# Keys transposed as two 64-row halves instead of one 128-row tile, in a gated linear attention and gMLP kernel

## The chip, the cores and the metric

The kernel runs on one NeuronCore of a Trainium2 chip. The metric is the device time of one execution in microseconds (us). Durations of single instructions are given in us or ns. The engines are PE (TensorE, matrix multiplies; its weight loads have rows of their own, PEld), DVE (VectorE), ACT (ScalarE), POOL (GpSimd) and SP (the queue that issues the DMAs). PE writes its results to PSUM, which has eight banks of 512 float32 columns in each partition; DVE and ACT carry them on to SBUF.

## The reference

There are 4 batches of 8 heads, 768 time steps and head size 48. The attention is a recurrence with a decay for each key dimension, and a gated MLP follows it:

```python
for t in range(S):                                             # q, k, v, alpha: (4, 8, 768, 48)
    state = alpha[:, :, t, :, None] * state + np.einsum('bhd,bhe->bhde', k[:, :, t], v[:, :, t])
    y[:, :, t] = np.einsum('bhd,bhde->bhe', q[:, :, t], state)
...
h = gelu(x @ w_in)                                             # x: y as (4, 768, 384); w_in: 384 x 1024
u, v = h[..., :512], h[..., 512:]
v_n = (v - mean(v)) / sqrt(var(v) + 1e-06) * g_ln
v_s = np.einsum('ts,bsd->btd', w_sg, v_n) + b_sg[None, :, None]
return x + (u * v_s) @ w_out
```

## The kernel before

The 768 steps of a batch are cut into 6 blocks of 128, so there are 24 blocks, numbered 0 to 23 here. The 8 heads stand as 4 pairs, and a pair takes 128 partitions, 64 for each of its heads (48 used). For block `i` DVE builds running products of the decays by two scans (`decay`, `invert`) and multiplies them into `q` and `k` (tile `kqv_t`).

What PE does for the attention comes in groups. Group `(o, i)` finishes the older block `o` and starts the newer block `i`, which is the next one. It has three steps, and on PE they stand one behind the other:

- `G` (`squares`): the scores of block `i` into tile `sc`, which has two PSUM banks, and the first part of the output `y` of block `o`. Block `o`'s contribution to the state goes to `dl0` (in the bank of tag `tp`) and to `dl1` (columns 256 to 447 of the second bank of `sc`).
- `M` (`squares_more`): the rest of block `o`'s output within the block, and the part from the old state `s_c`.
- `H` (`squares_end`): the part from the state at the middle of the block, `s_m`, and then, for block `i`, the transposes of the scaled keys. They are in float32, one of 128x128 for each of the four pairs, into the tile `tp`, which is one bank.

All matmuls of a group but the transposes are of 64x64, so that four of them run in the four quarters of the array at a time. `side_by_side` interleaves the lists of two row halves.

Around a group, DVE multiplies the scores by the causal mask (`causal`, tile `at`) and updates the state: `state_half` (`s_m`), then `state_add` and `state_decay` (`s_c`). ACT copies the transposed keys to SBUF (`k_rows`, tile `kn`), and the output to `xf` and `y3` (`x_rows`, `y_last`). Six small DMAs on SP then pack `y3` into `xf`, and ACT and DVE or POOL split `xf` into `xh` and `xl`, the operands of the MLP. Group `(i, i+1)` needs `at` and `kn` of block `i`.

The MLP is 128x128 work: `mm_v`, `mm_u`, `mm_s` and `mm_o` are its four products, in three passes each for float32 accuracy. The first 67 us also split the weights into two parts (`mm_w`).

The order of all this is made by a planner (`Plan`): every step is entered with its engine, a cost in ns, what it must follow, and the buffers it takes. `issue` then picks steps by their expected start and due time. The order on PE is mostly fixed by a list of units (`units`), in which the steps of a group are counted with the costs that `group` returns. The order on DVE, ACT, POOL and SP follows from the plan's costs. The framework under it adds semaphore waits: for data, and also between accesses by two engines to one PSUM tile; which of two such accesses waits is decided by the order in which the plan issued them.

Of the kernel before, what the change touches and what calls it, by code (L numbers as in the profile page):

```python
# [9 lines left out]
F32 = mybir.dt.float32  # L10
# [8 lines left out]
B, H, S, D = 4, 8, 768, 48  # L19
DM, DFF = 384, 1024  # L20
HALF = DFF // 2
P = 128
# [3 lines left out]
NP = H // 2  # L26
# [135 lines left out]
def tile_gla_gmlp(ctx: ExitStack, tc: tile.TileContext, aT, kqv, w_in, w_sgT, w_out, g_ln, b_sg, out):  # L162
    nc = tc.nc
# [4 lines left out]
    ps = ctx.enter_context(tc.tile_pool(name="ps", bufs=1, space=PSUM))  # L168
# [201 lines left out]
    def half(e):  # L370
        return slice(64 * e, 64 * e + 64)
# [34 lines left out]
    def gain_list(i, h):  # L406
# [6 lines left out]
            for j in range(NP) for e in range(2)  # L413
        ]

    def side_by_side(*slots):
        made = []
        for upper, lower in slots:
            for k in range(max(len(upper), len(lower))):
                made += [part[k]() for part in (upper, lower) if k < len(part)]  # L420
        return made
# [42 lines left out]
    def squares_end(o, i):  # L464
        if o is not None:
            side_by_side((inter_list(o, 1, 0), inter_list(o, 1, 1)))
        if i is not None:
            st[i]["tp"] = tp = ps.tile([P, NP, P], F32, tag="tp", name="tp")
            for j in range(NP):
                nc.tensor.transpose(tp[:, j], st[i]["k"][:, j], ident)  # L470

    def causal(i):
        s = st[i]
# [6 lines left out]
    def k_rows(i):  # L480
        s = st[i]
        s["kn"] = kn = att1.tile([P, NP, P], F32, tag="kn", name="kn")
        nc.scalar.copy(kn, s["tp"])

    def keep_warm(o, n):
        for _ in range(n):
# [253 lines left out]
    def group(o, i):  # L740
        i = i if i is not None and i < n else None
        name = ("G", o, i)
        if o is not None:
            o_at[o] = name
        if i is not None:
            s_at[i] = name
        first = [(name, 95 + SLOT * (2 if o is None else 3 if i is None else 5))]
        if o is not None:
            first.append((("M", o, i), 2 * SLOT))
        return first + [(("H", o, i), (0 if o is None else SLOT) + (0 if i is None else 530))]  # L750

    for i in range(NCH):
        units += group(i - 1 if i > 0 else None, i)
# [98 lines left out]
    for i in range(n):  # L852
# [14 lines left out]
        last = c == NCH - 1  # L867
        ended = ("H",) + o_at[i][1:]
        plan.add(("causal", i), "dve", 670, lambda i=i: causal(i), [s_at[i]], takes=[("at", 1, [o_at[i]])])
        plan.add(("kn", i), "act", 575, lambda i=i: k_rows(i), [("H",) + s_at[i][1:]], takes=[("kn", 1, [o_at[i]])])  # L870
        plan.add(
            ("half", i), "dve", 350, lambda i=i: state_half(i), [o_at[i]],
            lead={o_at[i]: SLOT * (0 if o_at[i][2] is None else 2)}, keen=400,
# [32 lines left out]
    for name, ns in units:  # L906
        if name[0] == "G":
# [2 lines left out]
            users = []  # L910
            if i is not None:
                deps += [("q", i), ("k", i)]
                users.append(("causal", i))
            if o is not None:
                deps += [("causal", o), ("kn", o)] + ([("state", o - 1)] if o % NCH > 0 else [])
                users += [("add", o)] if o % NCH < NCH - 1 else []
# [180 lines left out]
```

## Time and profile before

| | before |
|---|---|
| time, median of 3 runs | 375.91 us (375.25 to 377.3) |
| the profiled execution's own time | 374.54 us |
| its span in the trace | 372.8 us |
| mean granted PE clock | 0.988 |
| PE busy | 344.4 us, 92% |
| DVE busy | 265.1 us, 71% |
| ACT busy | 152.8 us, 41% |
| POOL busy | 60.6 us, 16% |

The profiled execution is 1.37 us under the median of the runs, and its time is 1.7 us more than its span. All single durations below come from that one execution. A row of a timeline gives the start, the length, the engine, the line, the operation, the tile written and the tiles read, and how many instructions the row merges; a bracket tells how long the engine had been idle and what released it.

### The profile page before, as it was taken

What the parts mean: (1) busy time and instruction counts of PE and PEld (TensorE: products, weight loads), DVE (VectorE), ACT (ScalarE), POOL (GpSimd) and SP (SyncE); (2) the same over time, 40 slices, a digit from 0 to 9 for tenths busy, and PEclk for the clock granted to TensorE, in tenths of its full rate; (3) what the DMA queues carried; (4) which work ended last, traced back from release to release, by engine and by line L of the source; (5) the groups of instructions that cost most, each with busy time, mean ns of one, the idle gap of its engine ahead of it and who ended that gap; (6) DMA issues with size and microseconds to landing.
All of it is one profiled execution on the core that took longest, in us unless ns stands there. A gap on an engine that the chain in (4) does not pass through costs nothing.

```text
span 372.8 us, 10703 instructions
## 1 busy us (share of the span) xinstructions
PE 344.4 (92%) x4480; PEld 314.3 (84%) x4480; DVE 265.1 (71%) x526; ACT 152.8 (41%) x367; POOL 60.6 (16%) x103
## 2 busy tenths in 40 slices
PE   2786989999998799999999999899999999999993
PEld 2554768799998798989999998699999989799983
DVE  4799997799996977888466887786577645443351
ACT  3285576755433344653312445543232335311010
POOL 1002133414201121320101301420111113300000
PEclk9999699999999999999999999999999999999998
DMA  8855675125356134531232344131221110000102
GB/s 304 281 195 139 218 250 181 42 73 163 98 170 205 31 111 122 162 114 37 66 117 93 119 138 136 52 101 28 92 83 73 30 50 8 1 2 0 63 3 70
DMA packets 18712, 39.38 MB, mean 106 GB/s; under 512 B 3936, under 2 KB 10848, under 8 KB 18656
## 3 DMA queue, kind: packets, MB, share of 16 engines
q1 hardware_dynamic: 18656, 38.61, 32.2%
q8 instruction: 37, 0.61, 0.7%
q14 instruction: 19, 0.16, 0.1%
HBM read 32.70 MB, written 4.72 MB: 100 GB/s over the span
## 4 chain that ended last, share of the span: by engine, by line
PE 68%; DVE 10%; DMA 8%; ACT 4%; SPq 4%; issue 3%; POOL 2%; DVEq 0%; ACTq 0%; POOLq 0%
PE mm_s L551 8%; PE mm_s L549 8%; PE mm_s L550 8%; DMA xf<-y 4%; PE mm_o L550 4%; PE mm_o L551 4%; PE mm_o L549 4%; PE mm_u L549 4%; SPq L520 4%; PE mm_u L551 4%; PE mm_u L550 4%; PE mm_v L549 3%; DMA kqv_t<-in_kqv 3%; PE mm_v L551 3%; PE mm_v L550 3%
## 5 line engine op out<-in xcount | busy, mean ns | idle before, releaser
L549 PE MATMUL mm_s<-ws_hi,vh 128*128 128x384 f32 x192 | 65.9, 343 | 1.3 <-ACT ws_hi L223 0.8
L550 PE MATMUL mm_s<-ws_lo,vh 128*128 128x384 f32 x192 | 65.1, 339 | 0.4 <-DVE ws_lo L226 0.4
L551 PE MATMUL mm_s<-ws_hi,vl 128*128 128x384 f32 x192 | 65.1, 339 | 0.1
L640 ACT CAST gh<-g 128x384 fp32r<-128x384 f32 x32 | 16.3, 512 | 57.9 <-DVE g L635 39.4
L630 DVE SCALAR_TENSOR_TENSOR g<-mm_s,g_col,b_bc 128x384 f32<-128x384 f32 x32 | 19.4, 608 | 26.1 <-PE mm_s L551 26.1
L549 PEld LDWEIGHTS mm_s<-ws_hi,vh 128*128 128x128 f32 x192 | 36.0, 188 | 2.1 <-ACT ws_hi L223 1.1
L550 PEld LDWEIGHTS mm_s<-ws_lo,vh 128*128 128x128 f32 x192 | 36.1, 188 | 0.8 <-DVE ws_lo L226 0.7
L551 PEld LDWEIGHTS mm_s<-ws_hi,vl 128*128 128x128 f32 x192 | 36.0, 188 | 0.4 <-DVE vl L596 0.4
L376 PE MATMUL sc<-kqv_t 64*64 64x64 f32 x768 | 27.8, 231 | 7.4 <-DVE kqv_t L361 4.7
L549 PE MATMUL mm_u<-xh,wi_hi 128*128 128x384 f32 x96 | 33.2, 346 | 0.1
L549 PE MATMUL mm_o<-gh,wo_hi 128*128 128x384 f32 x96 | 32.4, 338 | 0.3 <-ACT gh L640 0.3
L376 PEld LDWEIGHTS sc<-kqv_t 64*64 64x64 f32 x768 | 25.4, 146 | 8.5 <-DVE kqv_t L361 5.1
L550 PE MATMUL mm_o<-gl,wo_hi 128*128 128x384 f32 x96 | 32.4, 338 | 0.1
L550 PE MATMUL mm_u<-xl,wi_hi 128*128 128x384 f32 x96 | 32.5, 338 | 0.0
L551 PE MATMUL mm_u<-xh,wi_lo 128*128 128x384 f32 x96 | 32.4, 338 | 0.0
L551 PE MATMUL mm_o<-gh,wo_lo 128*128 128x384 f32 x96 | 32.3, 337 | 0.0
L549 PE MATMUL mm_v<-wi_hi,xh 128*128 128x512 f32 x72 | 30.3, 421 | 1.7 <-ACT u L615 1.4
L333 DVE TENSOR_TENSOR_SCAN pf<-a,floor 128x516 f32<-128x516 f32 x24 | 30.0, 1251 | 2.4 <-DMA a<-in_aT 2.2
L351 DVE TENSOR_TENSOR_SCAN pf<-a,floor 128x516 f32<-128x516 f32 x24 | 29.5, 1228 | 1.1 <-ACT pend L339 0.4
L551 PE MATMUL mm_v<-wi_hi,xl 128*128 128x512 f32 x72 | 28.5, 396 | 0.0
L550 PE MATMUL mm_v<-wi_lo,xh 128*128 128x512 f32 x72 | 28.4, 395 | 0.0
L389 PEld LDWEIGHTS y<-at,kqv_t 64*64 64x64 f32 x768 | 16.9, 141 | 13.2 <-issue 5.3
(109 smaller groups left out, 760.2 us busy)
## 6 DMA issues: line engine op xcount, KB each, us to landing
kqv_t<-in_kqv SPq DMA_DIRECT2D x24, 768.0 KB, 4.6
a<-in_aT SPq DMA_DIRECT2D x24, 258.5 KB, 2.7
out_x<-r SPq DMA_DIRECT2D x24, 192.0 KB, 2.5
raw<-in_w_in SPq DMA_DIRECT2D x8, 384.0 KB, 8.0
xf<-y SPq DMA_DIRECT2D x144, 8.0 KB, 2.7
raw<-in_w_out SPq DMA_DIRECT2D x4, 384.0 KB, 3.3
raw<-in_w_sgT SPq DMA_DIRECT2D x6, 192.0 KB, 2.4
raw_sg<-in_w_sgT SPq DMA_DIRECT2D x1, 768.0 KB
```

Source lines behind the costliest of these rows:

```text
L333: nc.vector.tensor_tensor_scan(pf.rearrange("p j t -> p (j t)"), s["a"][:, 0:NP * C1], floor.rearrange("p j t -> p (j t)"), initial=0.0, o ...
L351: nc.vector.tensor_tensor_scan(s["pf"].rearrange("p j t -> p (j t)")[:, ::-1], s["a"][:, NP * C1:0:-1], floor.rearrange("p j t -> p (j t)" ...
L376: lambda j=j, h=h: nc.tensor.matmul(sc[half(h), e, 64 * j:64 * j + 64], k[half(e), j, half(h)], q[half(e), j, half(h)], start=True, stop=True,
L389: lambda j=j: nc.tensor.matmul(y_of(y, j, e)[:, half(h)], v[half(h), j, half(e)], at[half(h), e, j], start=first and j < 2, stop=True, ski ...
L520: nc.sync.dma_start(xf[64 * e + D:64 * e + 64, kk, tsl], y3[64 * e + 16 * kk:64 * e + 16 * kk + 16, :])
L549: nc.tensor.matmul(o, lh, rh, start=(idx == 0), stop=False)
L550: nc.tensor.matmul(o, lh, rl, start=False, stop=False)
L551: nc.tensor.matmul(o, ll, rh, start=False, stop=(idx == n - 1))
L630: nc.vector.scalar_tensor_tensor(t["g"], t["o"], g_col[:, d:d + 1], b_bc[:, tsl], op0=ALU.mult, op1=ALU.add,)
L640: nc.scalar.copy(g["h"][:, d], t["g"])
```

## The change

Each pair's key tile is transposed in two halves by partition, 64 rows at a time. The upper half (head 0 of each pair) goes to `tp0`, which is columns 256 to 511 of the first bank of `sc`; the lower half goes to `tp1`, which is the old bank of tag `tp`. The two halves are interleaved, so that there are eight transposes of 64 rows to 128 output rows and 64 columns where there were four. `k_rows` copies them in two pieces, each 4x64 columns. In the plan, step `H` is counted with 260 ns in place of 530 for the transposes, the copy with 760 ns in place of 575, and the tile `sc` is held until `kn` is copied.

```diff
+    def rows_list(i, e):
+        k, tp = st[i]["k"], st[i]["tp1"] if e else st[i]["tp0"]
+        return [
+            lambda j=j: nc.tensor.transpose(tp[:, j], k[half(e), j], ident[half(e), half(e)]) for j in range(NP)
+        ]
+
...
-            st[i]["tp"] = tp = ps.tile([P, NP, P], F32, tag="tp", name="tp")
-            for j in range(NP):
-                nc.tensor.transpose(tp[:, j], st[i]["k"][:, j], ident)
+            st[i]["tp0"] = st[i]["sc"][:, 0, 256:512].rearrange("p (j d) -> p j d", d=64)
+            st[i]["tp1"] = ps.tile([P, NP, P], F32, tag="tp", name="tp")[:, :, 0:64]
+            side_by_side((rows_list(i, 0), rows_list(i, 1)))
...
-        nc.scalar.copy(kn, s["tp"])
+        nc.scalar.copy(kn[:, :, 0:64], s["tp0"])
+        nc.scalar.copy(kn[:, :, 64:P], s["tp1"])
...
-        return first + [(("H", o, i), (0 if o is None else SLOT) + (0 if i is None else 530))]
+        return first + [(("H", o, i), (0 if o is None else SLOT) + (0 if i is None else 260))]
...
-        plan.add(("kn", i), "act", 575, lambda i=i: k_rows(i), [("H",) + s_at[i][1:]], takes=[("kn", 1, [o_at[i]])])
+        plan.add(("kn", i), "act", 760, lambda i=i: k_rows(i), [("H",) + s_at[i][1:]], takes=[("kn", 1, [o_at[i]])])
...
-                users.append(("causal", i))
+                users += [("causal", i), ("kn", i)]
```

From group (6, 7) on the units stand on PE in the order they had; in the first blocks a few pieces of `mm_w` have moved. The order of the other engines has changed in many places.

The end of a group on PE, block 14. Before (names end in the number of the buffer; `y` from `s_m` is the last 64x64 part, `mm_u` the next unit):

```order
L399 MATMUL y_2646<-kqv_t_2122,s_m_100 64x64 [waits DVE_49]
L399 MATMUL y_2646<-kqv_t_2122,s_m_100 64x64 x7
L470 MATMUL tp_2719<-ident_78,kqv_t_2249 128x128 [waits PE_49]
L470 MATMUL tp_2719<-ident_78,kqv_t_2249 128x128 x3
L549 MATMUL mm_u_2726<-xh_2020,wi_hi_103 128x384
```

The same place after:

```order
L399 MATMUL y_2716<-kqv_t_2180,s_m_100 64x64 [waits DVE_49]
L399 MATMUL y_2716<-kqv_t_2180,s_m_100 64x64 x7
L419 MATMUL sc_2715<-ident_78,kqv_t_2312 128x64 [waits DVE_49]
L419 MATMUL tp_2789<-ident_78,kqv_t_2312 128x64 [waits PE_49]
L419 MATMUL sc_2715<-ident_78,kqv_t_2312 128x64
L419 MATMUL tp_2789<-ident_78,kqv_t_2312 128x64
L419 MATMUL sc_2715<-ident_78,kqv_t_2312 128x64
L419 MATMUL tp_2789<-ident_78,kqv_t_2312 128x64
L419 MATMUL sc_2715<-ident_78,kqv_t_2312 128x64
L419 MATMUL tp_2789<-ident_78,kqv_t_2312 128x64
L556 MATMUL mm_u_2799<-xh_2075,wi_hi_103 128x384
```

The first transpose into `sc` has a wait for DVE that was not there: the instruction waited for is the mask multiplication of the same block (`at_2779<-sc_2715`), which reads the bank the transpose writes. Nine of the 24 blocks have this wait (1, 3, 5, 10, 14, 15, 20, 21 and 23). In the other fifteen the plan issues the transposes first, and the mask multiplication waits for them, or for the first of the two copies.

DVE around the same block (`s_m` from `dl0` is `state_half`, `at` the mask multiplication, `gl` a step of the MLP, `s_m` from `sc` is `state_add`, `s_c` is `state_decay`). Before:

```order
L495 TENSOR_TENSOR s_m_100<-s_c_98,dl0_2647 128x4x48 [waits PE_49]
L475 TENSOR_TENSOR at_2709<-sc_2645,mask_85 128x512 [waits PE_49]
L645 TENSOR_TENSOR gl_2582<-g_2688,gh_2565 128x384 [waits Activation_49]
L500 TENSOR_TENSOR s_m_100<-s_m_100,sc_2645 128x4x48 [waits DVE_49,PE_49]
L503 TENSOR_TENSOR s_c_98<-s_m_100,pend_97 128x4x48 [waits DVE_49]
```

And after:

```order
L502 TENSOR_TENSOR s_m_100<-s_c_98,dl0_2717 128x4x48 [waits PE_49]
L481 TENSOR_TENSOR at_2779<-sc_2715,mask_85 128x512 [waits PE_49]
L652 TENSOR_TENSOR gl_2637<-g_2758,gh_2633 128x384 [waits Activation_49]
L507 TENSOR_TENSOR s_m_100<-s_m_100,sc_2715 128x4x48 [waits Activation_49]
L510 TENSOR_TENSOR s_c_98<-s_m_100,pend_97 128x4x48 [waits DVE_49]
```

The order is the same. `state_add` now waits for ACT: for the first copy of `kn`, which reads the other bank of the same tile `sc`.

DVE around block 17, where the transposes come first. Before (`pf` is a scan for the next block):

```order
L495 TENSOR_TENSOR s_m_100<-s_c_98,dl0_3184 128x4x48 [waits PE_49]
L333 SCALAR_TENSOR_TENSOR pf_3248<-a_3002,floor_91 128x516 [waits DMAHW6_49,DVE_49]
L475 TENSOR_TENSOR at_3263<-sc_3182,mask_85 128x512 [waits PE_49]
L500 TENSOR_TENSOR s_m_100<-s_m_100,sc_3182 128x4x48 [waits DVE_49,PE_49]
L347 RECIPROCAL floor_91<-pf_3248 128x4 [waits DVE_49]
```

And after:

```order
L502 TENSOR_TENSOR s_m_100<-s_c_98,dl0_3271 128x4x48 [waits PE_49]
L333 SCALAR_TENSOR_TENSOR pf_3336<-a_3080,floor_91 128x516 [waits DMAHW6_49,DVE_49]
L507 TENSOR_TENSOR s_m_100<-s_m_100,sc_3269 128x4x48 [waits DVE_49,Activation_49]
L481 TENSOR_TENSOR at_3371<-sc_3269,mask_85 128x512
L510 TENSOR_TENSOR s_c_98<-s_m_100,pend_97 128x4x48 [waits DVE_49]
```

`state_add` and the mask multiplication have changed places, and both now stand behind a wait for the first copy on ACT.

## The prediction

> **What bounds the kernel now.** I read the page's head, slices and chain first, then the busy time by stages, then who waited for whom on PE, then timelines of single groups.
>
> ```profile
> span 372.8 us, 10703 instructions
> PE   2786989999998799999999999899999999999993
> PEclk9999699999999999999999999999999999999998
> PE 68%; DVE 10%; DMA 8%; ACT 4%; SPq 4%; issue 3%; POOL 2%; DVEq 0%; ACTq 0%; POOLq 0%
> 0.00:67.00 67.00, 50.49 (x874) 39.17 (x874) 55.54 (x115) 37.65 (x95) 12.25 (x27) 0.95 0.66 218
> 67.00:130.00 63.00, 59.70 (x791) 55.44 (x790) 57.16 (x115) 31.09 (x75) 13.30 (x15) 1.00 0.38 116
> 130.00:340.00 210.00, 207.67 (x2670) 194.00 (x2671) 141.23 (x278) 81.05 (x192) 35.01 (x62) 1.00 0.24 77
> ```
>
> The stage rows give a stretch, its length, then the busy time of PE, PEld, DVE, ACT and POOL, the granted clock, and the DMA share and rate. From 130 us PE is busy 207.7 of 210 us: whatever lengthens or shortens PE's own row there moves the end. Between 67 and 130 us DVE is nearly as full (57.2 of 63). Before 67 us PE is idle for a quarter, and one slice has the clock at 0.6. What PE waits for from 60 us on (all rows sum to 5.7 us):
>
> ```profile
> PE y L389 <- ACT alo L454: 1.4, 1, 1.4
> PE mm_v L549 <- ACT u L615: 1.4, 1, 1.4
> ...
> PE mm_o L549 <- ACT gh L640: 0.3, 1, 0.3
> ```
>
> So there are two prices to find: PE time of a group with the new transposes, and any new wait that stands on PE. Blocks 6 to 23, 18 of the 24, lie after 67 us. This is the end of a group there, block 14:
>
> ```profile
> 183.03 0.41 PE L399 MATMUL y<-kqv_t,s_m 64*64 64x64 f32 x16
> 183.06 0.69 DVE L475 TENSOR_TENSOR at<-sc,mask 128x512 f32<-128x512 f32 x1 [0.38 <-PE y L389]
> 183.37 0.66 PE L470 MATMUL tp<-ident,kqv_t 128*128 128x128 f32 x4
> 183.78 0.42 PE L549 MATMUL mm_u<-xh,wi_hi 128*128 128x384 f32 x1
> 184.04 0.34 PE L550 MATMUL mm_u<-xl,wi_hi 128*128 128x384 f32 x1
> 184.07 0.59 ACT L483 COPY kn<-tp 128x512 f32<-128x512 f32 x1 [0.30 <-PE tp L470]
> 184.55 0.48 ACT L517 COPY xf<-y 128x384 f32<-128x384 f32 x1
> ```
>
> While PE transposes at 183.37, the mask multiplication on DVE has only just begun (183.06, and it lasts to 183.75). Before, the two touch different banks and overlap.
>
> **The transposes themselves.** How the four stand, taken apart at block 6 (loads, then the first transpose), with two other 64x64 groups:
>
> ```profile
> 73.58 0.33 PE L470 MATMUL tp<-ident,kqv_t 128*128 128x128 f32 x1
> 73.58 0.14 PEld L470 LDWEIGHTS tp<-ident,kqv_t 128*128 128x128 f32 x1
> 73.64 0.14 PEld L470 LDWEIGHTS tp<-ident,kqv_t 128*128 128x128 f32 x1
> 73.74 0.14 PEld L470 LDWEIGHTS tp<-ident,kqv_t 128*128 128x128 f32 x1
> 73.85 0.14 PEld L470 LDWEIGHTS tp<-ident,kqv_t 128*128 128x128 f32 x1
> 72.95 0.69 PE L376 MATMUL sc<-kqv_t 64*64 64x64 f32 x32
> 305.75 0.63 PE L410 MATMUL dl<-kqv_t,kn 64*64 64x48 f32 x16
> ```
>
> The first transpose is held 0.06 us (0.33 against 0.27 for the others, since four span 0.66) and they follow at 0.11. The keys are the weights, the identity streams. The change halves the stream to 64 columns and puts two row halves side by side, but each load still has 128 columns. The first two loads are 0.06 apart, so a load needs no more than that; I take it that the 128 streamed columns set the 0.11. A 64-column stream then goes at the 0.06 of the scores, whose 32 matmuls, four abreast, start over 0.41 us (0.69 less the 0.22 of one and the hold of 0.06): seven steps of 0.058.
>
> From the first transpose to the next unit's true start, before: 0.41, plus 0.08 by which `mm_u`'s first matmul is held (0.42 against 0.34), is 0.49. After, four rounds: 0.06 + 3 x 0.06 + a last stream of 0.05 is 0.29. But a change of the array's shape costs: the last matmul from `s_m` starts at 183.22 (183.03 + 0.41 - 0.22) and streams 0.05, and the first 128x128 transpose truly starts at 183.43, so 0.16 pass. From a 128x128 transpose to a 128x128 `mm_u` nothing passes: the last begins at 183.76 (183.37 + 0.66 - 0.27), takes 0.11, and `mm_u` truly begins at 183.86. Before, a group pays for the shape once here. Now the transposes are 64 rows by 128 columns, a third shape, which is left again for 128x128. The nearest row is the shape change that the trace shows, so I add 0.15: 0.44 after, against 0.49, a gain of 0.05 a block. If leaving the third shape is free, the gain is 0.20; if rounds take 0.11 as now, 0.06 + 0.33 + 0.05 + 0.15 = 0.59, a loss of 0.10. Over 18 blocks: **-0.9 us (-3.6 to +1.8)**.
>
> The Trainium skill, "TensorEngine Tiling (Array Packing)", section "Key Properties", says that a change of the tiling mode, unlike a change of tile, drains the array. The 0.16 and the nothing above agree with it; that 64x128 counts as a mode of its own no row here shows. By that rule the sum is the -0.9; with an exit that is free it would be -3.6.
>
> **The new wait on PE.** In nine blocks the transposes into `sc` wait until the mask multiplication has read that bank. In block 14 it ends at 183.75. From the end of a DVE step to a PE load that waited for it pass 0.07 us:
>
> ```profile
> 306.43 0.35 DVE L495 TENSOR_TENSOR s_m<-s_c,dl 128x192 f32<-128x192 f32 x1 [1.42 <-PE dl L410]
> 306.84 0.27 PEld L399 LDWEIGHTS y<-kqv_t,s_m 64*64 64x64 f32 x12
> ```
>
> So the transposes begin at 183.82 in place of 183.37: +0.45. Behind them in PE's queue stands the whole MLP unit, so nothing fills the gap, and the mask multiplication can't come earlier, since its release is PE's own first part of `M` (the bracket). Blocks 15, 20, 21 and 23 have the same pattern; here is the last one, and block 10, where DVE is later but so is PE:
>
> ```profile
> 300.37 0.69 DVE L475 TENSOR_TENSOR at<-sc,mask 128x512 f32<-128x512 f32 x1 [0.38 <-PE y L389]
> 300.69 0.66 PE L470 MATMUL tp<-ident,kqv_t 128*128 128x128 f32 x4
> 130.08 0.68 DVE L475 TENSOR_TENSOR at<-sc,mask 128x512 f32<-128x512 f32 x1
> 130.62 0.66 PE L470 MATMUL tp<-ident,kqv_t 128*128 128x128 f32 x4
> ```
>
> Five blocks at 0.45 and block 10 at 0.21 (130.83 for 130.62): **+2.5 us**. The lower bound is 1.2, if half of it falls into idle time that PE has later anyway; the upper 3.0, if a DVE step comes between.
>
> **The blocks where the transposes go first.** There the mask multiplication waits for the transposes or for ACT's first copy, and `state_add` for that copy too; DVE stands meanwhile. From 130 us DVE has 69 us of slack in 210, and `at` isn't needed before the next group, several MLP units later. I take 0 (0 to +1, for blocks 7 to 9 in the stretch where DVE is full).
>
> **The copies.** Sizes by their rows:
>
> ```profile
> L483 ACT COPY kn<-tp 128x512 f32<-128x512 f32 x24 | 14.1, 587 | 14.5 <-PE tp L470 14.3
> L517 ACT COPY xf<-y 128x384 f32<-128x384 f32 x24 | 11.6, 482 | 0.0
> L507 ACT COPY y<-y 128x128 f32<-128x128 f32 x24 | 6.6, 277 | 1.3 <-DMA xf<-y 1.3
> 220.79 0.59 ACT L483 COPY kn<-tp 128x512 f32<-128x512 f32 x1
> ```
>
> 128 to 384 columns cost 205 ns more, so 256 take 277 + 103 = 380 ns. `kn` and `xf` start 0.48 apart in block 14 though `kn` lasts 0.59, so copies overlap by 0.11: two halves hold ACT for 0.54, where one held it for 0.48. At 41% ACT hides +0.06. On the path it counts where `xf` waits behind `kn`: the chain goes through the row at 220.79, on to the DMAs of `xf` and, by way of ACT, to PE's 1.4 us wait. **+0.1 (0 to 0.3)**.
>
> **The first 67 us.** Here the path is not PE's row but goes from group to group. Rows for blocks 1 and 2:
>
> ```profile
> 17.03 0.69 DVE L475 TENSOR_TENSOR at<-sc,mask 128x512 f32<-128x512 f32 x1 [0.62 <-PE y L389]
> 17.32 1.11 PE L470 MATMUL tp<-ident,kqv_t 128*128 128x128 f32 x4
> 18.52 0.59 ACT L483 COPY kn<-tp 128x512 f32<-128x512 f32 x1 [2.92 <-PE tp L470]
> 28.24 0.66 DVE L475 TENSOR_TENSOR at<-sc,mask 128x512 f32<-128x512 f32 x1
> 28.32 0.66 PE L470 MATMUL tp<-ident,kqv_t 128*128 128x128 f32 x4
> ```
>
> Block 1 waits until 17.79 (17.03 + 0.69 + 0.07) for 17.32, +0.47; its transposes are at the lower clock and gain about 0.2 there; `kn` and all behind it on ACT move by the rest, +0.27. In block 2 the transposes go first: their last starts 0.24 after 28.32, lasts some 0.22, and with 0.04 to the release the mask multiplication starts at 28.82 for 28.24, +0.58, and the scan behind it on DVE is on the chain. The other early blocks I count at 0, since SP's DMAs are the path there. **+0.85**. But the plan has moved whole steps here: a `y3` copy, for which PE waits, now stands behind two more casts of 0.5 us, and elsewhere steps have gone forward. By such pieces the bounds are -1.5 and +3.
>
> **The sum.** -0.9 + 2.5 + 0.1 + 0.85 = +2.55 us: the profiled execution's 374.54 would become 377.1. That execution is 1.37 under the median of 375.91, so in terms of the median I forecast **378.4 us**.
>
> **Rivals.**
>
> *Loads set the rounds.* The `dl` group streams 48 columns and starts 16 matmuls, two abreast, over 0.41 (0.63 - 0.22): seven steps of 0.058, no faster than the 64-column scores. So something other than the stream can set a step, and loads of equal width are the obvious one. Against it stand the two loads 0.06 apart. Rounds then stay at 0.11: +1.8 in place of -0.9, the sum +5.25, 381.2 us. The Trainium skill, "TensorE: Matmul & The Clock Gate", section "LDWEIGHTS (loading the stationary operand)", has the rule that speaks for this one: the load's time goes by its columns, and 32 rows take as long as 128.
>
> *Leaving the third shape is free.* -3.6 in place of -0.9: the sum is -0.15, 375.8 us, no change.
>
> *The array keeps its shape on both sides*, because only its columns are rejoined: neither change costs. This is the one that ends faster. The twelve late blocks without a wait gain 0.20 + 0.15 = 0.35, the six with one 0.20, together -5.4, and the sum is -1.95, 374.0 us. It takes at least 0.35 a block; at 0.2 the waits eat it. For it speaks only that quarters of the array work independently; against it the 0.16 between 64x64 and 128x128.
>
> *The start decides.* The reordered first 67 us move by more than all the rest: -1.5 gives 376.0, +3 gives 380.5. If the stretch of half clock goes away or grows, the sign can be either.
>
> **Chances and range.** The forecast's terms 0.42, loads 0.15, free exit 0.17, shape kept 0.10, the start 0.16. What a measurement of this kernel can tell from no change is about 0.5%, 1.9 us. The forecast itself, spread by some 1.6 us for the start, is slower by more than that in two cases of three, and else the same. The loads are slower throughout, the free exit nearly always the same, the shape kept faster, the start half slower and a third faster. Together: slower 0.50, same 0.33, faster 0.17. The range leaves out one in ten on each side: 373.6 to 382.4. The forecast's own range is 376.5 to 380.5.
>
> **What would show it.** Right: transposes of 64 rows at 0.06 a pair, a gap of 0.15 before the next MLP matmul, a PE wait for `at` of about 0.4 us in blocks 14, 15, 20, 21 and 23, PE busy time lower by some microseconds. Wrong: pairs at 0.11, no gap behind them, no PE row that waits for the mask multiplication, or a first `mm_v` run (67.5 us before) that has moved by more than 1.5 us.

## The result, and the profile after

The changed kernel takes 386.72 us (median of 4 runs, 385.95 to 388.06), against 375.58 for the kernel before on the same chip: a ratio of 1.0328, 95% interval 1.0276 to 1.038. It is 11 us slower where I forecast 2.5. The profiled execution took 387.27 us, with a span of 385.6. (The ratios here leave out runs in which the clock was disturbed and the medians don't, so the two can differ by some tenths of a per cent.)

The page's head, the slices and the chain, and the three stages, to be laid beside those of before:

```profile
span 385.6 us, 10916 instructions
PE   2577399999898999999999999989999999999993
PEclk9989599999999999999999999999999999999999
PE 59%; DVE 22%; ACT 5%; issue 5%; DMA 3%; SPq 2%; POOL 2%; DVEq 0%; ACTq 0%; POOLq 0%
0.00:67.00 67.00, 44.12 (x870) 33.74 (x871) 50.03 (x102) 35.08 (x92) 7.40 (x21) 0.90 0.58 196
67.00:130.00 63.00, 59.25 (x691) 52.67 (x690) 56.62 (x119) 31.66 (x80) 12.29 (x16) 1.00 0.42 132
130.00:340.00 210.00, 205.03 (x2800) 188.02 (x2799) 142.84 (x281) 85.87 (x214) 30.53 (x60) 1.00 0.25 79
```

The damage is early. In the first 67 us PE is busy 44.1 us in place of 50.5 and DVE 50.0 in place of 55.5, at a mean clock of 0.90 in place of 0.95. In the chain DVE's share has gone from 10% to 22%. Between 130 and 340 us PE is busy for 2.6 us less.

The starts of the transposes of single blocks say where. They are read from the timelines, in us, of one execution each; the columns behind the first are differences to it, of experiments too, which are explained below. Block 6, which begins the second batch, is left out: units around it have changed places, and it starts only 2.2 us later in the changed kernel.

| block | before | after | old code, new order | halves in `y`, new order | halves, shared bank, old order | halves in `y`, old order |
|---|---|---|---|---|---|---|
| 1 | 17.32 | +1.0 | 0.0 | +0.3 | +0.9 | +0.8 |
| 2 | 28.32 | +2.2 | -0.8 | -0.5 | +3.3 | +0.6 |
| 4 | 41.65 | +6.9 | +2.6 | +4.1 | +5.0 | +1.9 |
| 7 | 90.11 | +8.8 | +6.7 | +4.1 | +4.8 | +2.2 |
| 9 | 111.09 | +9.3 | +6.7 | +4.1 | +5.6 | +2.4 |
| 13 | 163.32 | +9.2 | +6.2 | +4.5 | +7.6 | +7.0 |
| 14 | 183.37 | +10.7 | +7.0 | +5.4 | +8.4 | +7.0 |
| 18 | 226.90 | +11.3 | +7.0 | +5.4 | +9.8 | +7.0 |
| 23 | 300.69 | +12.5 | +6.8 | +4.4 | +10.5 | +5.4 |

(The last column has 4.0 us between blocks 9 and 11 from a stretch of half clock, 133 to 140 us, which this kernel's profiled execution had and the profile before had not.) Of the 12.5 us, 9.3 have come by block 9, and 3.3 come later.

The late part is what was forecast. Block 14 after, from the end of the group:

```profile
193.33 0.41 PE L399 MATMUL y<-kqv_t,s_m 64*64 64x64 f32 x16
193.36 0.69 DVE L481 TENSOR_TENSOR at<-sc,mask 128x512 f32<-128x512 f32 x1 [0.38 <-PE y L389]
194.11 0.27 PE L419 MATMUL sc<-ident,kqv_t 64*128 64x64 f32 x1 [0.36 <-DVE at L481]
194.22 0.22 PE L419 MATMUL sc<-ident,kqv_t 64*128 64x64 f32 x1
194.28 0.22 PE L419 MATMUL sc<-ident,kqv_t 64*128 64x64 f32 x1
194.34 0.22 PE L419 MATMUL sc<-ident,kqv_t 64*128 64x64 f32 x1
194.50 0.45 PE L556 MATMUL mm_u<-xh,wi_hi 128*128 128x384 f32 x1
194.60 0.37 ACT L489 COPY kn<-sc 128x256 f32<-128x256 f32 x1 [0.53 <-PE tp L419]
195.01 0.35 DVE L507 TENSOR_TENSOR s_m<-s_m,sc 128x192 f32<-128x192 f32 x1 [0.34 <-ACT kn L489]
```

The transposes stand behind the mask multiplication, which ends at 194.05; they start 0.78 after the `s_m` part (193.33), where before it was 0.34 (183.37 less 183.03): +0.44. Then the pairs follow at 0.11, 0.06 and 0.06, and `mm_u` truly starts at 194.61 (194.50, and 0.11 of the first matmul is hold). Below `kn`, `state_add` stands for ACT's first copy. Who waited, on PE (the first row up to 130 us, the others from there to 340; total, times, longest) and on DVE and ACT in the first 100 us:

```profile
PE y L389 <- ACT y L514: 9.0, 3, 7.3
PE sc L419 <- DVE at L481: 1.8, 5, 0.4
PE mm_s L556 <- ACT vh L599: 1.4, 3, 0.5
DVE s_m L507 <- ACT kn L489: 4.6, 4, 2.2
ACT kn L489 <- DVE at L481: 4.1, 2, 2.5
```

The five late PE waits are there; block 10 has a sixth, of 0.14 us. The prediction had put `state_add`'s wait for the copy at 0, it did not name the copy's wait for the mask multiplication, and the wait for `y3` in the first row it named, within a bound of 3 us for all the moved pieces.

### The profile page after: what moved, and what is told of

Read it like the earlier page. It is cut to its first block, busy times and chain, and to the rows that moved or that the text cites. A ratio compares the mean times of both kernels' runs of the same rounds, so it can differ in the third digit from the quotient of the medians.

```text
span 385.6 us, 10916 instructions
## 1 busy us (share of the span) xinstructions
PE 347.7 (90%) x4576; PEld 312.9 (81%) x4576; DVE 265.9 (69%) x528; ACT 157.9 (41%) x395; POOL 50.2 (13%) x97
## 4 chain that ended last, share of the span: by engine, by line
PE 59%; DVE 22%; ACT 5%; issue 5%; DMA 3%; SPq 2%; POOL 2%; DVEq 0%; ACTq 0%; POOLq 0%
PE mm_s L558 6%; PE mm_s L556 6%; PE mm_s L557 6%; PE mm_o L557 4%; PE mm_o L558 4%; PE mm_o L556 4%; PE mm_v L556 3%; PE y L389 3%; PE mm_v L558 3%; PE mm_v L557 3%; DVE at L481 3%; DVE pf L351 3%; DVE pf L333 2%; PE mm_u L556 2%; PE mm_u L557 2%
## 5 line engine op out<-in xcount | busy, mean ns | idle before, releaser
L389 PE MATMUL y<-at,kqv_t 64*64 64x64 f32 x768 | 22.7, 234 | 10.5 <-ACT y L514 9.0
```

Source lines behind the costliest of these rows:

```text
L389: lambda j=j: nc.tensor.matmul(y_of(y, j, e)[:, half(h)], v[half(h), j, half(e)], at[half(h), e, j], start=first and j < 2, stop=True, ski ...
```

## The experiments

### Code and order taken apart

The plan's three new numbers alone set the order; the new transposes and copies do not. With the numbers of before, the changed code is issued in exactly the order of before on every engine, and with the new numbers the old code in exactly the order of after. So code and order can be crossed. The first run has the new code with the old numbers:

```diff
-        return first + [(("H", o, i), (0 if o is None else SLOT) + (0 if i is None else 260))]
+        return first + [(("H", o, i), (0 if o is None else SLOT) + (0 if i is None else 530))]
-        plan.add(("kn", i), "act", 760, ...
+        plan.add(("kn", i), "act", 575, ...
-                users += [("causal", i), ("kn", i)]
+                users.append(("causal", i))
```

> The half transposes and two copies, with the plan's three numbers as they were before (530, 575, `sc` held by the mask multiplication alone). The plan then issues every step in exactly the order of before, on all engines; ten blocks (the nine and block 8) have the transposes wait for the mask multiplication. Theory A (the order that the new plan numbers made in the first 90 us costs the time): +2 to +3 us against before, about 378, which is the PE waits of 0.43 us in blocks 14, 15, 20, 21 and 23 and little else; the transposes of block 8 start within 2 us of before (100.7). Theory B (the shared bank holds up the chain of the first 90 us, whatever the order): +9 to +12 us, about 386, with block 8 at 108 us or later.

383.61 us against 375.71, ratio 1.0207 (1.0153 to 1.0262). The second has the old code with the new numbers, the same lines the other way round:

> The old transposes and the one copy, with the plan's new numbers (260, 760, `sc` held until `kn`). The plan issues every step in exactly the order of the changed kernel. Theory A (order): +7 to +9 us against before, about 383 to 385, block 8 at 108 us or later. Theory B (shared bank): within 1.5 us of before, block 8 within 2 us of 100.7.

381.17 us, 1.0137 (1.0075 to 1.0199). The third takes away the shared bank, in all blocks but 0 and 6, and keeps the order of after; the fourth does so in the order of before. (Both also hold `y` in the plan until `kn` is copied, which leaves the order as it is.)

```diff
-            st[i]["tp0"] = st[i]["sc"][:, 0, 256:512].rearrange("p (j d) -> p j d", d=64)
+            st[i]["tp0"] = (st[i]["sc"][:, 0, 256:512].rearrange("p (j d) -> p j d", d=64) if o is None
+                            else st[o]["y"][:, :, C:C + 64])
```

> The changed kernel in its own order, but the upper halves go to unused columns (128 to 191) of the output tile `y` of the older block, not into `sc` (blocks 0 and 6, which have no older block, keep `sc`). No transposes wait for the mask multiplication, and neither it nor `state_add` waits for ACT's copy. Theory A (order): -2 to -3.5 us against the changed kernel, about 383.5, block 8 still at 108 us or later. Theory B (shared bank): back to within 2 us of before, about 375 to 377. If the price of the late waits is right, the gain between blocks 13 and 23 alone is 2.2 us against the changed kernel under either theory.

380.47 us, 1.0115 (1.0057 to 1.0174).

> The half transposes with the upper halves in `y`, and the old plan numbers: the order of before exactly, no shared bank. Theory A and theory B both: the time of before within 1.5 us, since a block without a wait gains nothing (0.498 us from the first transpose to the next MLP matmul, against 0.494 before). If it is over 2 us slower, the halves or the two copies cost something by themselves; if over 1 us faster, the shorter transposes bring something in the first 67 us.

375.70 us, 1.0022 (0.9975 to 1.0069). Together, as ratios to before:

| | order of before | order of after |
|---|---|---|
| old transposes | 1 | 1.0137 |
| halves, upper ones in `y` | 1.0022 | 1.0115 |
| halves, upper ones in `sc` | 1.0207 | 1.0328 |

Neither theory was right alone; the parts add up. The halves and the two copies neither cost nor bring anything that can be told from nothing here (1.0022, with half a per cent on either side). The shared bank costs 1.9% in the old order (1.0207 less 1.0022) and 2.1% in the new one, 7 to 8 us. The new order costs 0.9 to 1.4%, 3.5 to 5 us. Each of these differences is uncertain by about 0.7 of a per cent. Of the shared bank's 7 to 8 us the late PE waits are about 3 in the profiles: between blocks 9 and 23 the changed kernel loses 3.3, and 0.3 with the upper halves in `y`.

### What the shared bank does in the first 100 us

This is the chain of the shared bank in the old order from 17 to 24 us (the chain of what ended last: start, length, what; pieces are left out at the marks):

```profile
17.47 0.69 DVE at L481
18.16 0.27 DVE mag L250
18.42 0.55 DVE top L254 x2
18.98 0.38 ACT kn L489
...
19.39 0.04 DVE s_m L507
...
19.66 0.56 DVE top L260
...
20.25 0.51 ACT wi_hi L263
...
21.91 1.28 PE mm_w L275 x2
```

The mask multiplication, ACT's copy and `state_add` have become links of one chain, and the weight splitting (`top`, `wi_hi`, `mm_w`) stands behind it. From the mask to the copy the view goes by `mag` and `top`, with which the copy has nothing to do; the transposes, which wait for the mask from 17.8 to 18.2 and end at 18.90, are the link that the code has there. So the chain goes from DVE to PE, ACT and back to DVE. With the upper halves in `y` the copy is still a link, the mask and `state_add` are not:

```profile
17.77 0.43 PE y L399 x15
18.20 0.29 PE y L419
...
18.91 0.37 ACT kn L490
19.28 0.27 ACT kn L491
...
20.11 0.50 ACT wi_hi L263
...
21.52 0.65 PE mm_w L275 x2
```

Laid side by side, the two chains also say how little of the delay is made in the ring itself. `wi_hi` starts 0.14 us later with the shared bank (20.25, 20.11), or 0.5 us later counted from the start of the group (14.99, 15.36). The transposes of block 2 start 2.7 us later, and the rest of that comes behind the ring: `mm_w` takes 1.28 us for 0.65, at half clock. More of this below.

To tell the waits apart, they were put back by hand into this version, some at a time, in the order of before. First all that has to do with the mask:

```diff
+            if "masked" in st[i]:
+                after(st[i]["rows"][0], [st[i]["masked"]])
...
+        if "rows" in s:
+            after(s["masked"], [s["c0"]] if "c0" in s else s["rows"][-1:])
...
+        if "masked" in s:
+            after(s["c0"], [s["masked"]])
```

(`masked` is the mask multiplication, `rows` the upper transposes, `c0` the first copy.)

> The version with the upper halves in `y` and the order of before (375.7, no different from before), to which the waits between the mask multiplication, the transposes and ACT's first copy are added by hand, as the shared bank makes them: the same ten blocks let the transposes wait for the mask; in the others the mask waits for the transposes, and the first copy then waits for the mask. `state_add` waits for nothing new. Theory A (these waits carry all that the shared bank costs): 382 to 384, as the shared bank itself in this order (383.6). Theory B (`state_add`, which has to wait for ACT's copy, carries the part of the first 90 us): about 379, which is the 3 us of the late PE waits alone.

383.35 us, 1.0231 (1.0141 to 1.0322): as much as the shared bank itself. Then `state_add` and the first copy alone:

```diff
+        if s["older"] is not None and "added" in st[s["older"]]:
+            after(s["c0"], [st[s["older"]]["added"]])
...
+        if "rows" in st.get(i + 1, {}):
+            after(st[i]["added"], [st[i + 1]["c0"]] if "c0" in st[i + 1] else st[i + 1]["rows"][-1:])
```

> The same base, with the other half of the waits: `state_add` and ACT's first copy are put in the order in which they are issued (in 18 blocks `state_add` waits for the copy), the mask multiplication waits for nothing new. Theory A: within 1 us of 375.7. Theory B: 379 to 381, with block 8 at 104 us or later.

377.17 us, 1.0079 (1.0032 to 1.0127). A smaller price, if it is one over the base (1.0022, up to 1.0069), and not needed for the whole: 1.0231 is reached without it. Next, of the mask's waits, the one on PE alone (the first of the three pieces):

> The version with the upper halves in `y` and the order of before (375.7), to which of the shared bank's waits only one kind is added: in the ten blocks 1, 3, 5, 8, 10, 14, 15, 16, 20, 21, 23 in which the mask multiplication is issued first (less the one where the bank isn't shared), the transposes wait for it on PE. Theory A (PE's waits are the price): 7 of 0.43 us late, the same in blocks 1, 3, 5 and 8, and the slower clock behind block 1: +5 to +8 us, 381 to 384. Theory B (the copy behind the mask is the price of the first 90 us): +3 us, 378 to 379.

380.71 us, 1.0170 (1.0117 to 1.0223). And the other two pieces without it:

> The same base with the other waits around the mask: in the other blocks the mask multiplication waits for the transposes, and in all blocks where the mask is issued first ACT's first copy waits for it. PE waits for no mask. Theory A: within 1.5 us of 375.7. Theory B: +4 to +5 us, 380 to 381. If both runs are over 4 us slower, the two kinds of wait add up to about the 8 us of both together; if the sum is well over 8, they overlap.

379.16 us, 1.0141 (1.0079 to 1.0203). Against before, the one kind of wait alone costs 6.4 us, the other 5.3, and both together 8.7. The base itself stands at 0.8, so over it these are 5.6, 4.5 and 7.9. That would be an overlap of 2 us, but with intervals of half to nearly one per cent it is not shown. (In the order of before the mask multiplication comes first in blocks 1, 3, 8, 10, 14, 15, 16, 20, 21 and 23 by the traces, and not in block 5.)

The second kind has its price early: its block 8 is 5.1 us late, where the base has 2.3, and behind that block it loses no more. It holds two waits together: the mask multiplication's for the transposes, which I priced at 0 because DVE "stands meanwhile", and the copy's for the mask, which I had not listed. In block 7 of this run both are seen, and below them the same place of the base:

```profile
95.41 0.69 DVE L483 TENSOR_TENSOR at<-sc,mask 128x512 f32<-128x512 f32 x1 [0.41 <-PE tp L419]
96.14 0.37 ACT L493 COPY kn<-y 128x256 f32<-128x256 f32 x1 [3.45 <-DVE at L483]
92.36 0.67 DVE L482 TENSOR_TENSOR at<-sc,mask 128x512 f32<-128x512 f32 x1
92.85 0.38 ACT L490 COPY kn<-y 128x256 f32<-128x256 f32 x1 [2.98 <-PE tp L419]
```

The transposes end at 95.38 and 92.82, so the copy comes 0.76 us behind them in place of 0.03.

Is there an order in which the bank can be shared for nothing? The mask multiplication was issued behind ACT's copies in all blocks:

```diff
+        for i in range(B * NCH):
+            names = [n for n, _ in made]
+            here, copy = names.index(("causal", i)), names.index(("kn", i))
+            if here < copy:
+                made.insert(copy, made.pop(here))
```

(`made` is the list of steps as the plan has ordered them.)

> The half transposes with the shared bank in the order of before (383.6), but in each block the mask multiplication is issued right behind ACT's copies of the keys. So PE never waits for the mask, the first copy never waits for the mask, and the mask waits for the first copy in all blocks. Theory A (the copy that stands behind the mask, and PE that stands behind it, are the price): 3 us back from the seven late waits of 0.43 us and 3 us or more in the first 90 us, 376 to 378. Theory B (any sharing of the bank costs, in whichever order, since DVE now stands until ACT has copied): 380 or more.

383.53 us, 1.0278 (1.0192 to 1.0365). Not this one; no other was run. The PE waits are gone, and in their place stands this row, on DVE:

```profile
DVE at L489 <- ACT kn L497: 13.1, 16, 2.5
```

### The order: a wait for y3

In the changed kernel PE waited 7.3 us for `y3` of block 2, in the old code with the new order 6.5, before 3.6. On ACT `y3` stood behind two `wi_hi` casts, so it was moved ahead of them, in the old code:

```diff
+MOVES = [(("xh", 1), ("pend", 5)), (("y3", 2), ("pend", 5))]
```

> The old transposes in the order of the changed kernel (381.2), and two steps of block 1 and 2 moved on ACT: the cast `xh` of block 1 and the copy `y3` of block 2 go ahead of the `pend` copy of block 5, which waits for a DVE scan, and so ahead of the two `wi_hi` casts. In the run before they ended at 40.60 us, and PE waited 6.5 us for `y3`; in the kernel before they ended at 37.97. Theory A (this piece of the order makes half of the order's cost, and it stays to the end): 2 to 3 us faster, 378 to 379, the PE wait down to about 4 us. Theory B (DVE's chain is as late as PE there, so the gain is given back by block 7): within 1 us of 381.2, with the wait shorter all the same.

381.30 us, 1.0205 (1.0133 to 1.0277): nothing gained, and PE's wait is still 6.5 us. ACT was not the cause. Its row, and SP's queue there:

```profile
40.05 0.51 ACT L538 CAST xh<-xf 128x384 fp32r<-128x384 f32 x1 [3.38 <-DMA xf<-y]
31.08 3.96 SPq L530 DMA_DIRECT2D xf<-y  x5
35.14 0.53 SPq L337 DMA_DIRECT2D kqv_t<-in_kqv  x1
35.71 0.51 SPq L530 DMA_DIRECT2D xf<-y  x1
```

Before, all six packs of block 1 were issued (30.18 to 35.13) ahead of this 768 KB load; the new plan puts the load between the fifth and the sixth. `xh`, which needs the sixth, then starts only at 40.05, 4.3 us after its issue, and `y3`, whose only buffer the packs read, isn't written earlier. The moves on SP and on ACT together, with the upper halves in `y` and then in the changed kernel itself:

```diff
+MOVES = [
+    (("pack", 1, 2, 1), ("kqv", 5)), (("xh", 1), ("pend", 5)), (("y3", 2), ("pend", 5)),
+]
```

> The changed kernel's order without the shared bank (upper halves in `y`, 380.5), with three steps moved: the sixth pack DMA of block 1 goes ahead of the 768 KB load of `kqv` for block 5 on SP, where it stood in the kernel before, and on ACT `xh` of block 1 and `y3` of block 2 go ahead of `pend` of block 5. The move on ACT alone, in the old code, changed nothing: there `xh` waited 3.4 us for the DMAs into `xf`. Theory A (the pack DMA that the plan put behind the big load is what holds up `y3`, and PE's clock falls for longer because of it): PE's wait for `y3` down from 7.8 to 4 to 5 us, half clock 6.8 us in place of 10.2, 3 to 4.5 us faster, 376 to 377.5. Theory B (the other moved pieces carry the order's cost): 379.5 or more.

378.44 us, 1.0128 (1.0059 to 1.0197). The wait is 5.4 us for 7.8, block 4 is 2.2 us earlier, and the median is 2.0 lower than that of the version without the moves, but the ratio is not (1.0115): by the times this is unclear.

> The changed kernel itself, the bank shared as it is, with the three moves: the sixth pack DMA of block 1 ahead of the 768 KB load for block 5 on SP, and `xh` of block 1 and `y3` of block 2 ahead of `pend` of block 5 on ACT. Theory A (the pack behind the load is a real part of the order's cost): PE's wait for `y3` down from 7.3 to 4 to 5 us, 2 to 3 us faster, 384. Theory B (the gain is given back, as with the filled clock): 386 or more.

386.28 us, 1.0336 (1.0284 to 1.0388), no gain. Here the wait has nearly halved, from 7.3 to 3.8 us, and it is given back on the spot:

```profile
41.34 0.25 ACT L526 COPY y<-y 128x128 f32<-128x128 f32 x1
42.49 0.20 ACT L351 COPY pend<-pf 128x4 f32<-128x4 f32 x1 [0.90 <-DVE pf L345]
44.24 0.98 ACT L275 CAST wi_hi<-top 128x384 fp32r<-128x384 f32 x2 [1.55 <-DVE top L272]
45.12 0.19 ACT L472 COPY alo<-alo 128x1 f32<-128x1 f32 x1
```

`y3` is there at 41.6, but the small copy `alo`, for which PE's next part waits, stands behind the `wi_hi` casts until 45.1, and these behind DVE's `top`. So DVE was as late there as the packs had been. The stretch of half clock from 39.5 us has grown as well, from 10.2 to 13.7 us.

### The clock

While PE stands for `y3` its clock falls to a half: before from 36.2 to 43.1 us, after from 39.3 to 49.5. The Trainium skill, "TensorE: Matmul & The Clock Gate", section "Part 1: The HAM clock gate", says that the clock is halved after an idle window of about 3.4 us and comes back after a busy one, and advises against such gaps. The lengths agree: the stretches last 3.4, 6.8 and 10.2 us. The idle window does not. By PE's rows it had been idle for 1.8 us when the clock fell before (34.43 to 36.24) and for 1.7 after (37.57 to 39.26), and in the changed kernel it also fell at 22.2 us, behind only 2.0 us of idle time (19.81 to 21.82).

The gap was filled, in both kernels, with matmuls that nobody reads (48 before, 112 after; they take one of the MLP's three PSUM buffers for the time):

```diff
+        if (o, i) == (3, 4):
+            fill(48)
```

> The kernel before, with 48 idle matmuls (the mask by itself, 128x128, into an accumulator that nobody reads) put on PE ahead of group (3,4), where PE waits 3.6 us for `y3`. They fill some 2.7 us of that wait and compute nothing that is used. Theory A (the stretch of half clock from 36.2 to 43.1 us comes from PE's idle time in that wait, and what PE does in it then takes twice as long): the stretch goes, and 1 to 2.5 us with it, 373 to 374.5. Theory B (the clock falls for another reason, or the chain there is not PE's): within 1 us of before.

> The changed kernel with 112 idle matmuls at the same place, where PE waits 7.3 us for `y3` (some 6.2 us of it filled). The wait itself stays. Theory A: the half clock from 39.3 to 49.5 goes, of which PE works 4.6 us, so 2 to 3 us faster, 384. Theory B: within 1 us of 386.7.

374.88 us against 374.12, ratio 0.9969 (0.9917 to 1.0020), and 387.68 us, 1.0402 (1.0339 to 1.0464). The half clock is gone there in both (the rows below are of the changed kernel, without the fill and with it; PE's busy time in the second holds the idle matmuls), and the time is not:

```profile
39.00:50.00 11.00, 5.12 (x139) 4.66 (x139) 9.26 (x21) 4.39 (x13) 1.98 (x1) 0.53 0.35 107
39.00:50.00 11.00, 10.32 (x243) 9.21 (x241) 10.57 (x24) 5.21 (x15) 2.00 (x1) 1.00 0.33 103
```

In the filled kernel before, block 4 is 0.9 us earlier, and by block 7 nothing of it is left. So PE's speed in that stretch does not set what follows. Behind block 1 it could be different. There full clock comes only at 26.6 us with the shared bank in the old order, at 20.6 with the halves in `y`, and the `mm_w` run stands on the chain (1.28 for 0.65 in the rows above):

```diff
+            if i == 1:
+                fill(18)
```

> The half transposes with the shared bank in the order of before (383.6), with 18 idle matmuls (1.9 us at the half clock) behind the transposes of block 1, where PE is idle from 19 to 21.2 us. In that kernel PE's clock came up to full only at 26.6 us, against 19.2 before, and the `mm_w` matmuls from 21.2 on ran at half speed. Theory A (PE's idle time behind the mask multiplication keeps the clock down, and this is the price of the shared bank in blocks 1 and 2): full clock by 23 us, block 2 at 29 to 30 us in place of 31.6, 1.5 to 2.5 us faster, 381 to 382. Theory B (the copies that stand behind the mask are the price): within 1 us of 383.6.

382.34 us, 1.0212 (1.0152 to 1.0272). Full clock came at 21.4 us, and block 2 at 29.39 in place of 31.60; in the profiled executions 2.4 us of that lasts to the end. But the ratio of the times is that of the unfilled kernel (1.0207). Unclear.

Nor is it shown that the shared bank kept the clock down. PE's idle time ahead of the `mm_w` run is 0.74 us with the shared bank, 0.68 with the halves in `y` and 1.02 before. And in the order of before, the start of block 2 goes with the time at which the clock first comes to full, whatever was changed:

| profiled execution | full clock from | block 2 |
|---|---|---|
| before | 19.2 | 28.32 |
| before, gap ahead of block 4 filled | 19.7 | 0.0 |
| before, two DVE steps left out (below) | 20.1 | -0.1 |
| halves in `y` | 20.6 | +0.6 |
| shared bank, filled behind block 1 | 21.4 | +1.1 |
| the copy's and the mask's waits, without PE's | 24.2 | +1.9 |
| `state_add`'s wait alone | 24.3 | +1.9 |
| shared bank, mask behind the copies | 24.5 | +2.5 |
| shared bank | 26.6 | +3.3 |
| the PE wait alone | 26.7 | +3.3 |
| no shared bank, two DVE steps run twice (below) | 27.0 | +3.5 |
| all the mask's waits | 27.1 | +3.6 |

The times of full clock are from the profile's record of the clock. The clock column of the busy-time rows doesn't show them: for the first 20 us it gives 1.00 both before and with the shared bank in the old order.

So at block 2 the delay in the profiles is mostly PE's work at half clock. Whether the added waits bring that about or the moment at which an execution runs, one execution of each can't tell. It is a rival to the ring for the early part of the shared bank's price that these runs leave open; against it stands only that the filled kernel's times are no better.

### Is DVE the bound of the start?

What goes with the delay in all these profiles is DVE. Busy time in the first 100 us (PE, PEld, DVE, ACT, POOL, clock, DMA), in turn before, the halves in `y` in the old order, the shared bank in the old order, after:

```profile
0.00:100.00 100.00, 83.19 (x1263) 69.09 (x1267) 86.81 (x182) 57.62 (x140) 22.43 (x39) 0.97 0.54 176
0.00:100.00 100.00, 80.02 (x1199) 66.30 (x1200) 84.56 (x177) 57.34 (x144) 20.93 (x38) 0.97 0.53 176
0.00:100.00 100.00, 80.64 (x1185) 64.93 (x1186) 80.85 (x170) 55.79 (x141) 18.99 (x37) 0.97 0.54 175
0.00:100.00 100.00, 75.08 (x1162) 60.10 (x1163) 79.02 (x163) 52.40 (x131) 18.56 (x36) 0.93 0.50 167
```

DVE's missing time, 2.2, 6.0 and 7.8 us, is nearly block 8's delay, 2.3, 5.6 and 9.3. Before, DVE was busy 29.1 of the 30 us from 20 to 50:

```profile
20.00:50.00 30.00, 25.11 (x553) 19.30 (x553) 29.12 (x56) 19.11 (x52) 3.60 (x2) 0.89 0.56 180
```

If DVE sets the end of that stretch, its work must count as its standing does. Two of its steps were run twice:

```diff
-        plan.add(at("clamp"), "dve*", 330, p["clamp"], [at("size")])
+        plan.add(at("clamp"), "dve*", 330, (lambda p=p: (p["clamp"](), p["clamp"]())) if on_pe else p["clamp"], [at("size")])
...
+        plan.add(at("sign"), "dve*", 550, (lambda p=p: (p["sign"](), p["sign"]())) if on_pe else p["sign"], [at("shift")])
```

> The kernel before, in its order, with two DVE steps of each of the eight `w_in` pieces run twice (`clamp`, 0.35 us, and `sign`, 0.61 us; both give the same result when repeated): 7 us more of DVE work in the first 80 us, once the overlap of neighbours is taken off. Theory A (DVE is the bound of the first 100 us): block 8 and the end 5 to 7 us later, about 380. Theory B (the path goes by PE, its clock and the DMAs; DVE is one of many): within 2 us of before.

378.54 us, 1.0117 (1.0057 to 1.0178): 3 to 4.4 us for 6.6 us of work (DVE is busy 271.7 us in all for 265.1), and 5.5 at block 8. But 3.5 of the 5.5 are there at block 2, with the late full clock of the table above, so the profile does not part DVE's length from the clock. And they were left out, in the kernel before and in the changed one; these kernels leave out the sign and the lower bound of `w_in` and return other numbers:

> The kernel before, in its order, without the same two DVE steps of the eight `w_in` pieces (so the sign and the lower bound of w_in are left out of its first part): 7 us less DVE work. Theory A: 3 to 6 us faster, 369 to 371; less than the full 7, since PE, with 83 us busy in the first 100, comes next. Theory B: within 2 us of before.

> The changed kernel without the same two steps. Theory A: 4 to 7 us faster than the changed kernel, 380 to 382, since DVE there stands for others and has the more to catch up. Theory B: within 2 us of 386.7.

375.32 us, 1.0048 (0.9996 to 1.0101), and 385.49 us, 1.0308 (1.0243 to 1.0373): nothing, and 1.2 us by the medians with overlapping intervals. So DVE is not the only bound of the start. Some 7 us more of work there cost 3 to 4.4; as much less buys nothing. The likely reason is that other chains (PE with its waits for `y3` and for `ws_hi`, SP's loads and packs, ACT) are as long, but no run shows that. DVE's missing busy time is a measure of the delay, and not by itself its cause.

## Why the prediction was wrong

**The sign was right, the size was not:** +2.5 us forecast, +11 measured. Point by point:

- *Rounds of 0.06* was right: 0.11 to the first, then 0.06 and 0.06. *An exit that costs 0.15* was a little low: the last pair starts at 194.34 and streams 0.05, `mm_u` truly starts at 194.61, so it costs about 0.2. With that the gain of 0.05 a block is none: with the upper halves in `y`, blocks 14 to 18 and 20 to 23, in which nothing else differs, stay within 0.02 us of the distances of before. The term -0.9 is 0. The Trainium skill, "TensorEngine Tiling (Array Packing)", section "Key Properties", has the drain at a change of the mode; the trace agrees, and adds the 0.2 that it takes from 64x128 to 128x128 here. The three rivals on the array (rounds of 0.11, a free exit, a kept shape) are out.
- *The PE wait, +2.5,* was right: 0.44 in block 14, and about 3 us in all of the late part.
- *The copies, +0.1,* had the right size: in block 3 of the changed kernel `xf` starts 0.53 us behind the first copy (37.95, 38.48), where the prediction had 0.54 for 0.48. What they cost in time is under what these runs can tell: in the old order with the upper halves in `y`, 0.2% with half a per cent on either side.
- *The blocks where the transposes go first: 0 (0 to +1)* is the first step that failed. With the mask's waits but without PE's the kernel is 1.4% slower, 5 us, or 4.5 over its base, and nearly all of it comes by block 8. I had followed the mask multiplication, which waits for the transposes, and `state_add`, which waits for the copy. That the copy in its turn waits for the mask, where the plan issues the mask between the transposes and the copy, I had not listed; it closes the ring from DVE to ACT to DVE. And the slack that I gave DVE was that of the time behind 130 us. How much of the 5 us the waits make themselves, and how much the half clock that came with them in the profile (1.9 us at block 2), stays open.
- *The first 67 us: +0.85 (-1.5 to +3)* is the second, and the larger. The delay at block 7 was 8.8 us. The step "the other early blocks I count at 0, since SP's DMAs are the path there" was wrong: blocks 3 to 5 are 3.3, 6.9 and 6.0 us later. A stage row of 67 us with 55.5 us of DVE hid that DVE was full from 20 to 50. The bound of +3 came from single moved pieces; the order alone made 6.7 us there in the old code's profile, and 0.9 to 1.4% in the times.
- The piece that I named for the order, `y3` behind two casts, was a symptom. The packs behind a load on SP held it up, a queue whose order the prediction had not looked at, and when both were put right in the changed kernel the time was the same, and ACT's `wi_hi` and DVE's `top` were then as late. Which moved pieces carry the order's 3.5 to 5 us is not settled by these runs. It was not tried to undo them one engine at a time.
- The rival *the start decides* had the right place and stopped at +3. The stretch of half clock that it named did grow, from 6.8 to 10.2 us, but with it filled the time was the same.

No version beat the kernel before. The halves with no shared bank and the old order equal it within the interval.

## What to carry to other kernels

Before a PSUM tile is given a second use, list every pair of engines that touches it in a round, in the order of issue: here mask, transposes, copy and state update became one ring, and two parts of it alone cost 1.7 and 1.4%, where all of the mask's waits together cost 2.3. Free columns of `y`, which at that time only PE writes and only ACT reads, took the same data at no cost that could be measured. When a change edits both code and a planner's numbers, cross the two, in four runs; the parts added up here within some tenths of a per cent. In a stretch where several engines are nearly full, do not price a new wait at 0 nor a saving at its length: here 6.6 us more work on DVE cost 3 to 4.4, and 5.8 us less bought nothing. Look at windows short enough to show which engine is full.

## What the hardware showed that I had not expected

- Half clock in a stretch where PE waits cost nothing that could be measured, though PE's work there took nearly twice as long (the group of block 4 takes 3.6 us from its first `y` to its transposes in the changed kernel, 44.88 to 48.50, and 2.0 with the gap filled, 45.20 to 47.22): 10.2 us of it removed in the changed kernel, 6.8 in the kernel before, and neither was faster.
- The clock fell behind idle times of PE of 1.7 to 2.0 us, in the three places given above.
- In both runs of the old code in the new order PE stood 2.4 us in the middle of the `s_m` part of a group, up to 54.7 us in one and 55.6 in the other, with no releaser in the trace, and a stretch of half clock followed at 55.1 and 56.8. A row of this length is in no profile of the old order:

```profile
PE y L399 <- issue: 2.4, 1, 2.4
```

It is part of the 6.7 us at block 7 in that column, and one reason why a delay at one block of one profiled execution is not a price.
